# One weight load cut into transfers of 8, 8 and 112 partitions in a DMA-bound decode kernel

## The chip, the cores and the metric

The kernel runs on one core of a Trainium2 chip. The metric is the device time of the program in microseconds (us), the median of several executions. Each kernel was timed against the kernel before on the same chip.

The names in the profiles: PE is the matmul engine (PEld its weight loads), DVE, ACT and POOL are the vector, scalar and general engines, and SP is the engine that issues the loads here. The loads are carried out by the core's 16 DMA engines in packets, one contiguous row for one partition each: the trace of the kernel before has 15744 packets of 32 KB, 128 for each of its 123 loads of 4 MB, in sixteen rows in which one packet follows the other (from 165 to 200 us no gap is over 14 ns). SBUF is the memory on the chip that the loads write to, with 128 partitions. The DMA share is the mean busy share of the 16 DMA engines.

## The reference, cut to what matters

One token of a pre-LN decoder block with a cached attention of 32 heads and a dense layer behind it:

```python
B, Sq, D = 1, 1, 512
H, Sk, Dh = 32, 32768, 128          # k_cache, v_cache: [1, 32, 32768, 128] bf16
h  = x + attention(layernorm(x), k_cache, v_cache, wq) @ wo     # wo: [4096, 512] bf16, 4 MB
h2 = h + mish_mlp(layernorm(h), w1, b1, w2)
```

K and V are 537 MB of the 548 MB that are read. There is next to no reuse, so the kernel is a long stream of loads.

## The kernel before

SP issues all loads in one fixed order. K and V of a head come as 4 MB loads (128 partitions, 32 KB of contiguous memory for each); PE transposes K, multiplies, and frees the buffer for a later load. `wo` is loaded once, early, between a K and a V load, and stays.

```python
        def issue(ld):
            # ... src: 128 rows of up to 32 KB, dst: 128 partitions of the ring
            S.dma(SP, lambda: sp.dma_start(dst, src).then_inc(sems[ld.chan], 16), waits=ld.after)

            # ... in load_weights(which)
            elif which == "wo":
                S.dma(SP, lambda: sp.dma_start(
                    wo_sb[:, :, :], A_wo.rearrange("(h k) n -> k h n", k=128)).then_inc(sems["wo"], 16))
        # ...
        order = [(ld.pos, ld) for ld in loads]
        order += [(-1.0, "wqa"), (GH - 0.5, "wqb"), (GH + 2 * LAG + 0.2, "wo"),
                  (2 * GH + 2 * LAG + 0.2, "w12"), (1e9, "late")]
```

`wo_sb` has k, the place inside a head, on the partitions: partition k takes row k of each of the 32 heads, which are 32 pieces of 1 KB. On 16 engines that is 256 pieces for each. The first use of `wo` is in `y_init`, which PE reaches at 95 us, long after `wo` has landed at 77 us:

```python
            S.step(PE, lambda: t_.matmul(yrow[:, :], oneb[0:1, 0:1].to_broadcast([1, 128]), xrow[0:1, :], ...),
                   waits=["consts", ("xr", 16), ("wo", 16)])
```

Of the kernel before, what the change touches and what calls it, by code (L numbers as in the profile page):

```python
# [9 lines left out]
ALU = mybir.AluOpType  # L10
ACTF = mybir.ActivationFunctionType
AXX = mybir.AxisListType.X

PE, ACT, DVE, POOL, SP = "pe", "act", "dve", "pool", "sp"
# [7 lines left out]

W1A = 5
W2A = 6

LAG = 8

# [175 lines left out]
def build_kernel(nc, A_x, A_k_cache, A_v_cache, A_wq, A_wo, B_w1, B_b1, B_w2, out, NE=4):  # L203
# [21 lines left out]
    def sb(shape, dt, name):  # L225
        cm = nc.sbuf_tensor(name, shape, dt)
        t = cm.__enter__()
        allocs.append(cm)
        return t.ap()
# [9 lines left out]
    wo_sb = wo_flat.rearrange("p (h n) -> p h n", h=H)  # L239
# [28 lines left out]
    wbar = sb([128, 1], F32, "wbar")  # L268
# [51 lines left out]
    sems = {e: sem(f"ev_{e}") for e in (PE, ACT, DVE, POOL, SP)}  # L320
# [20 lines left out]
    def program(S):  # L341
        t_ = nc.tensor
        a = nc.scalar
        v = nc.vector
        g_ = nc.gpsimd
        sp = nc.sync
# [12 lines left out]
        def load_weights(which):  # L359
            if which == "wqa":  # L360
                S.dma(SP, lambda: sp.dma_start(  # L361
                    wqa, A_wq[:, 0:NH0 * Dh].rearrange("(p kc) n -> p kc n", kc=KC)).then_inc(sems["wqa"], 16))
            elif which == "wqb" and H > NH0:
                S.dma(SP, lambda: sp.dma_start(
                    wqb, A_wq[:, NH0 * Dh:HD].rearrange("(p kc) n -> p kc n", kc=KC)).then_inc(sems["wqb"], 16))
            elif which == "wo":
                S.dma(SP, lambda: sp.dma_start(
                    wo_sb[:, :, :], A_wo.rearrange("(h k) n -> k h n", k=128)).then_inc(sems["wo"], 16))
            elif which == "w12":
                S.dma(SP, lambda: sp.dma_start(  # L370
                    w1v[:, :, 0:W1A * 128],
                    B_w1.rearrange("(kc p) f -> p kc f", p=128)[:, :, 0:W1A * 128]).then_inc(sems["w1a"], 16))
            elif which == "late":
                S.dma(SP, lambda: sp.dma_start(
                    w1v[:, :, W1A * 128:F],
                    B_w1.rearrange("(kc p) f -> p kc f", p=128)[:, :, W1A * 128:F]).then_inc(sems["w1b"], 16))
                for a_, b_, s_ in ((0, W2A, "w2a"), (W2A, FJ - 1, "w2b")):
                    S.dma(SP, lambda a_=a_, b_=b_, s_=s_: sp.dma_start(
                        w2v[:, a_:b_, :],
                        B_w2[a_ * 128:b_ * 128, :].rearrange("(j p) n -> p j n", p=128)).then_inc(sems[s_], 16))  # L380
                S.dma(SP, lambda: sp.dma_start(
                    w2v[0:FLAST, FJ - 1, :], B_w2[(FJ - 1) * 128:F, :]).then_inc(sems["w2c"], 16))
# [4 lines left out]
        for _, ld in sorted(order, key=lambda o: o[0]):  # L387
            if isinstance(ld, str):
                load_weights(ld)
            else:  # L390
                issue(ld)
        S.dma(SP, lambda: sp.dma_start(out[0, 0, :].rearrange("(g n) -> g n", g=4), outsb[0:128:32, :]).then_inc(sems["out"], 16),
              waits=["fin"])
# [14 lines left out]
        for k, done in (("k", f"kf{NK - GH - 1}"), ("v", f"pv{NK - 2 * GH - 1}")):  # L408
            for x in range(NX):
# [22 lines left out]
               name="ident", waits=["iota"])  # L432
# [118 lines left out]
        def y_init():  # L551
            S.step(PE, lambda: t_.matmul(
                yrow[:, :], oneb[0:1, 0:1].to_broadcast([1, 128]), xrow[0:1, :], start=True, stop=False,
                skip_group_check=True), waits=["consts", ("xr", 16), ("wo", 16)])


        CV = (GH - LAG) * R
# [76 lines left out]

        hl = H - 1
        y_init()
        if H > NH0:
            S.wait(DVE, ["qT"])
        S.step(DVE, lambda: v.tensor_reduce(wbar[:, :], wo_sb[:, hl, :], AXX, ALU.add), waits=[("wo", 16)], name="wbar")
        S.step(DVE, lambda: v.tensor_scalar_mul(wbh[:, 0:1], wbar[:, :], 1.0 / D), name="wbh0", waits=["wbar"])  # L640
        S.step(DVE, lambda: v.scalar_tensor_tensor(
            wbh[:, 1:2], wbar[:, :], 1.0 / D, wbh[:, 0:1], ALU.mult, ALU.subtract), name="wbh", waits=["wbh0"])
# [3 lines left out]
        for t in range(GH):  # L646
            group(H, t)
            if t == LAG + 5:
                S.step(DVE, lambda: v.tensor_reduce(ysum[:, :], yrow[:, :], AXX, ALU.add), name="ysum",
                       waits=[f"yr{hl - 1}"])  # L650
                S.step(DVE, lambda: v.tensor_scalar_mul(MEANH, ysum[:, :], 1.0 / D), name="meanh", waits=["ysum"])

                for c in range(KC):
                    S.step(DVE, lambda c=c: v.tensor_tensor(
                        yrs[:, c * 128:(c + 1) * 128], yrow[:, c * 128:(c + 1) * 128], ident[:, :], ALU.mult),
                        waits=[f"yr{hl - 1}"], name=(f"yrs" if c == KC - 1 else None))
                S.step(DVE, lambda: v.tensor_reduce(
                    ycol[:, :], yrs[:, :].rearrange("p (c n) -> p c n", c=KC), AXX, ALU.add), name="ycol", waits=["yrs"])
            if t == LAG + 9:
                S.step(PE, lambda: t_.matmul(YC, ident[:, :], ycol[:, :], start=True, stop=False,  # L660
                                             skip_group_check=True), waits=["ycol"])
                S.step(PE, lambda: t_.matmul(T_b[0][:, 0:FP], b1r[:, :], identb[0:FP, 0:FP],
                                             is_transpose=True, start=True, stop=True),
                       name="b1t", waits=[("b1", 32), f"ev{NK - 2}", f"ev{NK - 1}"])
                S.step(DVE, lambda: v.tensor_copy(b1T[:, :], T_b[0][:, 0:FJ]), name="b1T", waits=["b1t"])
        for t in range(LAG):
# [5 lines left out]
            name="oT", waits=[f"pv{NK - 1}", f"o1s{hl}"])  # L672
        y_cols(hl)
        for s in range(2):
# [3 lines left out]
                waits=(["wbh"] if s == 0 else ()), name=("ym" if s == 1 else None))  # L678
        S.step(DVE, lambda: v.tensor_scalar(HC, YC, YM, MEANH, ALU.subtract, ALU.subtract),
               name="hc", waits=["ym"])  # L680
# [4 lines left out]
        for j in range(FJ):  # L685
            W = 128 if j < FJ - 1 else FLAST
            for kc in range(KC):
# [3 lines left out]
                    name=("hid" if j == FJ - 1 and kc == KC - 1 else None),  # L691
                    waits=(["xcT", ("w1a", 16), f"exq{H - 1}"] if j == 0 and kc == 0
                           else [("w1b", 16)] if j == W1A and kc == 0 else ()))
            if j == FJ // 2:
                S.step(PE, lambda: t_.matmul(V_REG, onesm[:, :], SSQ2, start=True, stop=True), name="v2",
                       waits=["ssq2"])
        S.step(ACT, lambda: a.activation(LNV2, V_REG, ACTF.Ln, bias=EPSC), name="ln2", waits=["v2"])
        S.step(ACT, lambda: a.activation(RSTD2, LNV2, ACTF.Exp, scale=-0.5), name="rstd2", waits=["ln2"])
        for c in range(KC):
# [5 lines left out]
               name="z", waits=["hid", "rstd2", "b1T"])  # L705
# [7 lines left out]
        for j in range(FJ):  # L713
            W = 128 if j < FJ - 1 else FLAST
            waits = ["act"] if j == 0 else []
            if j in (0, W2A, FJ - 1):
                waits.append(({0: "w2a", W2A: "w2b"}.get(j, "w2c"), 16))
            for c in range(KC):
# [3 lines left out]
                    name=("y2" if j == FJ - 1 and c == KC - 1 else None), waits=(waits if c == 0 else ()))  # L722
        S.step(DVE, lambda: v.tensor_copy(outsb[:, :], yps[:, HROW:HROW + 128]), name="fin", waits=["y2"])

    program(_Sched(nc, False, events, sems))
    with nc.Block() as blk:
        counts = {}
        for eng_name, attr in ((POOL, "gpsimd"), (SP, "sync"), (DVE, "vector"), (ACT, "scalar"), (PE, "tensor")):
            emitter = _Sched(nc, True, events, sems, only=eng_name)

            def _run(eng, emitter=emitter):
                program(emitter)
            getattr(blk, attr)(_run)
            counts.update(emitter.cnt)
        check = _Sched(nc, False, {}, sems)
        program(check)
        assert counts == check.cnt, (counts, check.cnt)
# [31 lines left out]
```

## Time and profile before

| | before |
|---|---|
| time, median | 1288.61 us (4 runs, 1288.39 to 1288.80) |
| DMA, mean over the span | 426 GB/s |
| PE, DVE busy | 80%, 59% |
| one 4 MB load in steady state | every 9.71 us |
| `wo`, 4 MB in 1 KB pieces | 11.85 us |
| last V landing, then to the end | 1277.35 us, then 9 us |

These are lines of the page of the kernel before: busy time by engine, the DMA share in 40 slices (tenths) and the rate in GB/s in the same slices, the summary of packets, the chain of work that ended last, and the issues of the large loads with their size and time to landing.

```profile
PE 1027.5 (80%) x25072; PEld 994.2 (77%) x25103; DVE 759.4 (59%) x1353; ACT 34.0 (3%) x134; POOL 2.7 (0%) x12
...
DMA  9999999999999999999999999999999999999998
GB/s 375 424 409 426 428 435 428 436 428 435 428 435 429 434 430 432 431 433 431 433 431 432 430 434 430 433 430 434 430 431 433 431 433 431 433 430 433 431 419 324
...
DMA 57%; PE 38%; DVE 3%; issue 1%; SPq 0%; ACT 0%
...
ring<-in_A_k_cache_dram SPq DMA_DIRECT2D x62, 4096.0 KB, 22.6
ring<-in_A_v_cache_dram SPq DMA_DIRECT2D x61, 4096.0 KB, 20.8
...
wo_sb<-in_A_wo_dram SPq DMA_DIRECT2D x1, 4096.0 KB, 36.8
```

The DMA slices are full from end to end, no compute engine is, and the rate is flat at about 431 GB/s: the loads bound the kernel. (The PE part of the chain is work that runs while the next loads arrive.) A load lands about 21 us after its issue at 9.7 us per load, so two are in hand all the time, and the engines are never short of work.

The columns after the stretch are busy us and instructions of each engine, then the granted PE clock, the DMA share and the rate in GB/s.

```profile
62.00:72.00 10.00, 6.66 (x153) 6.64 (x153) 4.51 (x8) 0.00 (x0) 0.00 (x0) 0.83 1.02 336
72.00:92.00 20.00, 6.54 (x159) 6.41 (x157) 4.27 (x8) 0.00 (x0) 0.00 (x0) 0.66 1.05 429
200.00:400.00 200.00, 163.24 (x4034) 158.26 (x4036) 122.10 (x213) 4.94 (x20) 0.00 (x0) 0.91 1.00 431
```

(The share can stand a little over 1, here 1.02 and 1.05: the records of packets overlap.) The first stretch holds most of `wo`: 4 MB in 11.85 us is 354 GB/s instead of 431; the 1 KB pieces cost 2.1 us. What SP did (start, duration, issue):

```profile
39.95 0.33 SPq L357 DMA_DIRECT2D ring<-in_A_k_cache_dram  x1
40.33 0.43 SPq L367 DMA_DIRECT2D wo_sb<-in_A_wo_dram  x1
46.21 24.93 SPq L357 DMA_DIRECT2D ring<-in_A_v_cache_dram  x1
71.18 0.43 SPq L357 DMA_DIRECT2D ring<-in_A_k_cache_dram  x1
```

The V issue behind `wo` stood for 24.9 us (the trace shows the time, not the reason). That was still in time: the first packets of V started at 74.1 us, and the last piece of `wo` ended at 76.6.

Each of these transfers leaves sixteen completion updates in the trace, as many as there are engines. I read them as one per engine (the fetch below moves one engine and one update by the same 1.6 us), and they show more than a landing time. In order of time, us, for three loads of the kernel before (worked out from the trace):

```
K before wo   62.79 62.86 62.87 63.02 63.03 63.04 63.25 63.26 64.38 64.47 64.51 64.55 64.67 64.73 65.29 65.31
V behind wo   84.36 84.39 84.40 84.56 84.60 84.82 84.85 85.93 86.08 86.13 86.17 86.25 86.27 86.81 86.84 87.58
last V        1272.05 1272.11 1272.12 1272.58 1272.72 1272.85 1273.73 1275.24 1275.44 1275.75 1275.95 1276.16 1276.57 1276.59 1277.34 1277.35
```

From V behind `wo` on, seven engines are early and nine late, by up to 5 us. The distance does not shrink in any later load (3.2 us from first to last update here, 4.8 after 180 us, 5.2 to 5.3 at the end): every engine is full. It grows with fetches of instructions: the trace counts 20 of 16 KB, 17 of them before 200 us, each a packet of 1.07 us (median) in the row of one engine. The updates before and after the fetch at 177.5 us differ by one engine that fell back from 3.2 to 4.8 us behind the first. In the row of packets the fetch takes 1.10 us and the 32 KB packet behind it 1.68 instead of 1.22, together the 1.6 us. That these fetches cause the rest of the lag is read from the times. A useful quantity follows: the mean of the sixteen updates of V behind `wo`, less the mean of K before `wo`, less 9.71 us for V itself, is what `wo` cost an engine on average. Before, it is 12.0 us (11.85 us and a share of the fetches).

### The profile page before, as it was taken

How to read it: one execution, taken by the hardware profiler on the slowest of the kernel's cores; microseconds unless marked ns; L12 is line 12 of the kernel's file. 1: busy time of each engine (PE TensorE's matmuls, PEld its weight loads, DVE VectorE, ACT ScalarE, POOL GpSimd, SP SyncE). 2: the span in 40 equal slices, each digit the busy share in tenths (PEclk: the TensorE clock that was granted, in tenths of full speed). 3: DMA queues.
4: the chain of work that ended last, by engine and by line, in shares of the span. 5: the costliest groups of instructions: out<-in, count | busy, mean ns of one | idle time of the engine just before them, and what ended most of it. 6: DMA issues, size and time to landing. Idle time of an engine off the chain costs nothing.

```text
span 1286.6 us, 52403 instructions
## 1 busy us (share of the span) xinstructions
PE 1027.5 (80%) x25072; PEld 994.2 (77%) x25103; DVE 759.4 (59%) x1353; ACT 34.0 (3%) x134; POOL 2.7 (0%) x12
## 2 busy tenths in 40 slices
PE   6858787788787788788888778888877887877886
PEld 6747787788787787777887777877777877777885
DVE  5635565566565565665666655655655655656663
ACT  0000000000000000000000000000000000000000
POOL 0000000000000000000000000000000000000000
PEclk8878989988899988988989988989989989989996
DMA  9999999999999999999999999999999999999998
GB/s 375 424 409 426 428 435 428 436 428 435 428 435 429 434 430 432 431 433 431 433 431 432 430 434 430 433 430 434 430 431 433 431 433 431 433 430 433 431 419 324
DMA packets 28800, 548.45 MB, mean 426 GB/s; under 512 B 2696, under 2 KB 9704, under 8 KB 10984
## 3 DMA queue, kind: packets, MB, share of 16 engines
q1 hardware_dynamic: 28680, 548.09, 99.7%
q8 instruction: 20, 0.33, 0.1%
q14 instruction: 4, 0.03, 0.0%
q0 software_dynamic: 96, 0.00, 0.0%
HBM read 548.08 MB, written 0.00 MB: 426 GB/s over the span
## 4 chain that ended last, share of the span: by engine, by line
DMA 57%; PE 38%; DVE 3%; issue 1%; SPq 0%; ACT 0%
DMA ring<-in_A_k_cache_dram 56%; PE tps L477 20%; PE sps L500 8%; PE ops L530 8%; DVE kt L488 2%; DMA ring<-in_A_v_cache_dram 2%; PE hlp L599 1%; DVE scb L580 1%; PE hlp L582 1%; DVE pmax L578 1%; PE hlp L587 1%; SPq L357 0%; PE sps L688 0%; PE yps L719 0%; SPq L361 0%
## 5 line engine op out<-in xcount | busy, mean ns | idle before, releaser
L488 DVE COPY kt<-tps 128x1024 bf16<-128x1024 bf16 x1024 | 707.8, 692 | 494.0 <-PE tps L477 486.9
L477 PE MATMUL tps<-identb,ring 128*128 128x128 bf16 x8192 | 693.7, 234 | 179.4 <-DMA ring<-in_A_k_cache_dram 176.1
L477 PEld LDWEIGHTS tps<-identb,ring 128*128 128x128 bf16 x8192 | 523.8, 104 | 188.4 <-DMA ring<-in_A_k_cache_dram 182.6
L530 PE MATMUL ops<-pbuf,ring 128*128 128x32 bf16 x8192 | 361.7, 178 | 57.2 <-DMA ring<-in_A_v_cache_dram 55.7
L500 PE MATMUL sps<-qcur,kt 128*128 128x32 bf16 x8192 | 376.0, 180 | 11.0 <-DVE scb L580 7.1
L500 PEld LDWEIGHTS sps<-qcur,kt 128*128 128x128 bf16 x8192 | 328.6, 99 | 18.7 <-DVE scb L580 14.4
L530 PEld LDWEIGHTS ops<-pbuf,ring 128*128 128x128 bf16 x8192 | 281.6, 97 | 70.1 <-DMA ring<-in_A_v_cache_dram 59.1
L590 ACT ACTIVATE pbuf<-scb,nbias 128x192 bf16<-128x192 f32 x32 | 14.6, 455 | 1164.8 <-PE ops L530 1094.8
L599 PE MATMUL hlp<-esum,onesf 128*128 128x1 f32 x128 | 18.6, 249 | 0.1
L599 PEld LDWEIGHTS hlp<-esum,onesf 128*128 128x128 f32 x128 | 16.8, 190 | 0.0
L578 DVE TENSOR_REDUCE pmax<-sps 128x1 f32<-128x256 f32 x32 | 13.3, 415 | 0.5 <-PE sps L500 0.5
L580 DVE COPY scb<-sps 128x256 f32<-128x256 f32 x32 | 13.3, 415 | 0.0
L582 PE MATMUL hlp<-ident,pmax 128*1 128x128 f32 x64 | 13.1, 289 | 0.1
L594 ACT ACTIVATE pbuf<-scb,nbias 128x64 bf16<-128x64 f32 x32 | 11.1, 348 | 60.2 <-PE ops L530 60.2
L587 PE MATMUL hlp<-gmax,onesr 1*128 1x1 f32 x64 | 12.1, 256 | 0.1
L617 DVE TENSOR_SCALAR o1s<-ops,rtot 128x1 f32<-128x1 f32 x32 | 6.7, 210 | 8.0 <-PE ops L530 8.0
L587 PEld LDWEIGHTS hlp<-gmax,onesr 1*128 1x128 f32 x64 | 9.4, 182 | 1.2 <-DVE gmax L585 0.2
L607 DVE COPY qcur<-qT 128x1 bf16 (+1 forms) x63 | 9.3, 147 | 0.0
L585 DVE TENSOR_REDUCE gmax<-hlp 1x1 f32<-1x128 f32 x32 | 8.6, 270 | 0.2
L621 DVE SCALAR_TENSOR_TENSOR ocur<-ops,rtot,o1s 128x1 bf16<-128x1 f32 x31 | 6.6, 213 | 0.7 <-PE ops L530 0.7
L443 PE MATMUL hlp<-xnT,ring 128*128 128x1 bf16 x128 | 3.7, 164 | 3.1 <-issue 3.1
L443 PEld LDWEIGHTS hlp<-xnT,ring 128*128 128x128 bf16 x128 | 3.6, 99 | 3.2 <-issue 3.2
(85 smaller groups left out, 55.2 us busy)
## 6 DMA issues: line engine op xcount, KB each, us to landing
ring<-in_A_k_cache_dram SPq DMA_DIRECT2D x62, 4096.0 KB, 22.6
ring<-in_A_v_cache_dram SPq DMA_DIRECT2D x61, 4096.0 KB, 20.8
ring<-in_A_v_cache_dram SPq DMA_DIRECT2D x9, 1024.0 KB, 19.8
ring<-in_A_k_cache_dram SPq DMA_DIRECT2D x5, 1024.0 KB, 15.5
wo_sb<-in_A_wo_dram SPq DMA_DIRECT2D x1, 4096.0 KB, 36.8
ring<-in_A_wq_dram SPq DMA_DIRECT2D x1, 3584.0 KB, 30.4
ring<-in_A_k_cache_dram SPq DMA_DIRECT2D x1, 2048.0 KB, 12.1
ring<-in_A_v_cache_dram SPq DMA_DIRECT2D x1, 2048.0 KB, 21.2
```

Source lines behind the costliest of these rows:

```text
L477: S.step(PE, lambda r=r: t_.matmul(tb[:, r * 128:(r + 1) * 128], block("k", i, r), identb[:, :], is_transpose=True, start=True, stop=True) ...
L488: dve(i, lambda: v.tensor_copy(kt[:, i % NE, :], T_b[i % 2][:, :]), f"ev{i}", waits)
L500: S.step(PE, lambda r=r, c=c: t_.matmul(S_b[:, c:c + WIDE], kt[:, i % NE, r * 128:(r + 1) * 128], q.to_broadcast([128, WIDE]), start=True, ...
L530: S.step(PE, lambda r=r, c=c: t_.matmul(ob[:, 0:WIDE], block("v", i, r), pbuf[:, c:c + 1].to_broadcast([128, WIDE]), start=(r == 0 and g i ...
L578: dve(i, lambda: v.tensor_reduce(pmax[:, :], S_b[:, 0:NCOL], AXX, ALU.max), f"pmax{hs}", [f"qkb{hs}"])
L580: dve(i, lambda: v.tensor_copy(scb[:, :], S_b[:, 0:NCOL]), f"sc{hs}", [])
L582: S.step(PE, lambda: t_.matmul(A_REG, pmax[:, :], ident[:, :], start=True, stop=True), name=f"A{hs}", waits=[f"pmax{hs}"] + (["qT" if H > ...
L587: S.step(PE, lambda: t_.matmul(B_REG, onesr[0:1, :], gmax[0:1, :], start=True, stop=True), name=f"B{hs}", waits=[f"gmax{hs}"], priv=pe_cha ...
L590: S.step(ACT, lambda: a.activation(pbuf[:, 0:CV], scb[:, 0:CV], ACTF.Exp, bias=nb[:, :], scale=SC, accum_out=esum[:, 0:1]), name=f"exp{hs} ...
L594: S.step(ACT, lambda: a.activation(pbuf[:, CV:NCOL], scb[:, CV:NCOL], ACTF.Exp, bias=nb[:, :], scale=SC, accum_out=esum[:, 1:2]), name=f"e ...
L599: S.step(PE, lambda s=s: t_.matmul(C_REG, onesf[:, :], esum[:, s:s + 1], start=(s == 0), stop=(s == 1)), name=(f"C{hs}" if s else None), w ...
L607: S.step(DVE, lambda j=j, n=n: v.tensor_copy(qcur[:, j:j + 1], qT[:, n:n + 1] if S.round is None else qT[:, bass.ds(S.round + (3 - j), 1)] ...
```

## The change

Its intent rests on a premise that the kernel before does not show: eight partitions are moved by eight engines, both times the same eight, and 112 evenly by all sixteen. Two transfers of eight partitions then give eight engines 64 pieces more, and the 112 partitions left give each of the sixteen 32 pieces fewer. The texts call these eight the lower engines and the others the upper ones; these are only names for the two halves. If the late engines are the other eight, they gain 32 pieces of 46 ns, 1.5 us (an estimate, from 11.85 us for 256 pieces). Nothing else changes; the diff, with its context cut and two equal edits of the waits shown as one:

```diff
+WOP = 16
@@
             elif which == "wo":
-                S.dma(SP, lambda: sp.dma_start(
-                    wo_sb[:, :, :], A_wo.rearrange("(h k) n -> k h n", k=128)).then_inc(sems["wo"], 16))
+                for p0, p1 in [(p, p + 8) for p in range(0, WOP, 8)] + [(WOP, 128)]:
+                    S.dma(SP, lambda p0=p0, p1=p1: sp.dma_start(
+                        wo_sb[p0:p1, :, :],
+                        A_wo.rearrange("(h k) n -> k h n", k=128)[p0:p1]).then_inc(sems["wo"], 16))
@@ y_init and the reduction of wo_sb[:, hl, :] (wbar)
-                waits=[... ("wo", 16)]
+                waits=[... ("wo", 16 * (WOP // 8 + 1))]
```

More of the change, by code (lines that the diff above doesn't have):

```diff
@@ L553, in y_init @@
                 yrow[:, :], oneb[0:1, 0:1].to_broadcast([1, 128]), xrow[0:1, :], start=True, stop=False,
-                skip_group_check=True), waits=["consts", ("xr", 16), ("wo", 16)])
+                skip_group_check=True), waits=["consts", ("xr", 16), ("wo", 16 * (WOP // 8 + 1))])
         CV = (GH - LAG) * R
@@ L638, in program @@
             S.wait(DVE, ["qT"])
-        S.step(DVE, lambda: v.tensor_reduce(wbar[:, :], wo_sb[:, hl, :], AXX, ALU.add), waits=[("wo", 16)], name="wbar")
+        S.step(DVE, lambda: v.tensor_reduce(wbar[:, :], wo_sb[:, hl, :], AXX, ALU.add), waits=[("wo", 16 * (WOP // 8 + 1))], name="wbar")
         S.step(DVE, lambda: v.tensor_scalar_mul(wbh[:, 0:1], wbar[:, :], 1.0 / D), name="wbh0", waits=["wbar"])
```

## The prediction

> **What bounds the kernel now.** The DMA engines. The page's slices show them at nine tenths or more all but the last slice, 426 GB/s on average, with PE busy 80% and DVE 59%; the chain of waits is 57% DMA. In steady state one 4 MB load lands every 9.71 us. Each transfer has sixteen completion updates in the trace, one per engine. They show two groups: at the load that lands around 222 us seven come within 0.5 us and nine 2.6 to 4.8 us after the first; at the last value load they come at 1272.05-1273.73 (seven) and 1275.24-1277.35 us (nine). The lag comes from instruction fetches: the table of queues counts 20 of 16 KB; 17 of them lie before 180 us, and each costs the engine that serves it about 1.5 us, never caught up, because every engine is always full. The last value update, 1277.35 us, starts the tail (9 us to the end). So the time is the work of the slowest engine. Perfect balance would give about 2.5 us.
>
> **What the change does.** SP issues two transfers more (0.43 us each, SP has time); the bytes are the same. [...] wo took 11.85 us for 256 pieces of 1 KB per engine, 46 ns each. Lower engines get 288 pieces (+1.5 us), upper ones 224 (-1.5 us). That is the intent: if the fetches burden the upper half, it takes 1.5 us from the late engines. One late engine (2.6 us, delayed by other fetches) would be in the lower half, so the gain would be only 0.6 us.
>
> **Why I expect a loss.** [...] One engine here already moves 32 KB in 1.213 us, 27 GB/s[...]. From the early group's 1272.05-1273.73 us, and the one late lower engine, the last value update moves to about 1281-1283 us: +5 us; if the lower half is the late one, +8 us. All of it lies on the critical path.
>
> **Time:** 1294 us, 8 in 10 between 1287 and 1298.5. Chances: faster by over 2% 0.01, within 2% 0.97, slower 0.02.
>
> **What would show it.** [...]the 1 KB packets of the first two transfers last or stand about 150 ns apart per engine instead of 46; the first two transfers complete about 10 us after the load before them, on eight engines; afterwards eight updates of each load stay some 5 to 9 us behind the others; the last value update at 1281-1283 us; tail unchanged. [...]
>
> **What would make it wrong.** [...]starving of the upper engines[...].

Passages of this text and of the expectations below are cut, and each cut is marked. Terms of the forecast's sum went with them. The sum was: the eight lower engines need 20 us for `wo` instead of 11.85, +8.2 us, and stay late. Of the 20 us, 10.3 are 224 pieces of 46 ns, and the rest is a time that I assumed for the two small transfers, because I took eight neighbouring partitions to be slow together. The early group's last update, 1273.73 us, and 8.2 us give the 1281 to 1283 us of the text, +5 us. If neighbours are not slow, 1287.5 to 1290 us; and, as a risk, 1 to 2 us more if the 112 partitions are slow too.

## The result, and the profile after

| | before | after |
|---|---|---|
| time, median of 4 | 1288.61 us | 1302.16 us (1300.98 to 1302.30) |
| ratio | | 1.0102, 95% interval 1.0087 to 1.0117 |
| what `wo` cost an engine on average | 12.0 us | 22.9 us |
| last V landing | 1277.35 us | 1290.09 us |

Ratios are the mean time of one kernel's runs over that of the other's of the same rounds, so not quite the ratio of the medians. The change costs 13.5 us by the medians; in the two profiled executions (1288.37 and 1300.98 us) it is 12.6 us.

The page of the kernel after, the same lines:

```profile
PE 1032.2 (79%) x25103; PEld 996.8 (77%) x25103; DVE 759.3 (58%) x1353; ACT 34.0 (3%) x134; POOL 2.7 (0%) x12
...
DMA  9999999999999999999999999999999999999997
GB/s 375 412 265 425 431 431 431 431 434 432 431 430 435 432 430 430 435 432 431 430 435 431 431 431 434 432 431 431 434 432 431 431 433 433 432 430 433 432 418 313
...
DMA 57%; PE 38%; DVE 3%; issue 1%; SPq 0%; ACT 0%
...
ring<-in_A_k_cache_dram SPq DMA_DIRECT2D x62, 4096.0 KB, 22.4
ring<-in_A_v_cache_dram SPq DMA_DIRECT2D x61, 4096.0 KB, 20.1
...
wo_sb<-in_A_wo_dram SPq DMA_DIRECT2D x1, 3584.0 KB
...
wo_sb<-in_A_wo_dram SPq DMA_DIRECT2D x2, 256.0 KB
```

One slice of forty is different: the third, 65 to 97 us, falls from 409 to 265 GB/s. The DMA share of that slice is still full. This is the line to learn from: the engines were busy, but their packets took longer (89 ns for the median 1 KB packet of `wo`, 51 before). A hole in the share, as the 0.22 of e3 below, would have meant missing work; a full share at a lower rate means slow work. By stretches, after:

```profile
62.00:72.00 10.00, 4.50 (x104) 4.40 (x101) 2.77 (x5) 0.00 (x0) 0.00 (x0) 0.83 1.05 172
72.00:92.00 20.00, 5.46 (x127) 5.25 (x122) 4.21 (x7) 0.00 (x0) 0.00 (x0) 0.72 1.11 257
200.00:400.00 200.00, 165.11 (x4035) 159.71 (x4033) 121.85 (x214) 5.39 (x22) 0.00 (x0) 0.90 1.00 432
```

172 GB/s in the first ten us against 336, then 257 against 429 in the next twenty, and from 200 us on the same rate as before. These two deficits add up to 5.1 MB, 11.8 of the 12.6 us at 431 GB/s, so nearly all of the loss is made between 62 and 92 us, and it is never made good. SP, after:

```profile
39.62 0.33 SPq L359 DMA_DIRECT2D ring<-in_A_k_cache_dram  x1
39.99 16.39 SPq L371 DMA_DIRECT2D wo_sb<-in_A_wo_dram  x3
56.42 23.44 SPq L359 DMA_DIRECT2D ring<-in_A_v_cache_dram  x1
79.91 0.43 SPq L359 DMA_DIRECT2D ring<-in_A_k_cache_dram  x1
```

The completion updates of `wo` after the change, all three transfers together, and those of V behind it:

```
wo            40.49 40.89 66.24 66.39 66.75 67.27 67.54 68.92 69.19 69.39 69.56 69.58 70.07 70.39 70.89 71.91 72.82 73.19
              82.15 82.94 83.12 83.26 84.21 84.36 84.63 85.48 86.36 86.86 87.10 88.10 89.05 89.24 89.48 91.25
V behind wo   95.44 95.54 95.67 95.95 96.12 96.28 96.96 97.18 97.46 97.79 98.07 98.41 98.82 98.99 99.32 100.75
```

There are 34 updates, not 48: two at once after the issues (40.49 and 40.89 us) and 32 landings, which is 8 + 8 + 16. The kernel waits for a count of 48, and it was reached with these 34. Eight landings for each small transfer, where each full one has sixteen: so I read that the small transfers run on eight engines, as meant, and both are through by 73.19 us. But the 112 partitions then take until 82 to 91 us, on all sixteen engines. On average an engine spent 22.9 us on `wo`, 10.8 more than before; not just eight of them.

### The profile page after: what moved, and what is told of

Same layout as the page of the kernel before. It is cut to its first block, busy times and chain, and to the rows that moved or that the text cites. A ratio compares the mean times of both kernels' runs of the same rounds, so it can differ in the third digit from the quotient of the medians.

```text
span 1299.2 us, 52436 instructions
## 1 busy us (share of the span) xinstructions
PE 1032.2 (79%) x25103; PEld 996.8 (77%) x25103; DVE 759.3 (58%) x1353; ACT 34.0 (3%) x134; POOL 2.7 (0%) x12
## 4 chain that ended last, share of the span: by engine, by line
DMA 57%; PE 38%; DVE 3%; issue 1%; SPq 0%; ACT 0%
DMA ring<-in_A_k_cache_dram 56%; PE tps L482 20%; PE sps L505 8%; PE ops L535 8%; DVE kt L493 2%; DMA ring<-in_A_v_cache_dram 2%; PE hlp L604 1%; PE hlp L587 1%; DVE scb L585 1%; DVE pmax L583 1%; PE hlp L592 1%; PE yrow L552 1%; SPq L359 0%; PE sps L693 0%; PE yps L724 0%
## 5 line engine op out<-in xcount | busy, mean ns | idle before, releaser
L592 PE MATMUL hlp<-gmax,onesr 1*128 1x1 f32 x64 | 12.1, 256 | 0.1
L552 PE MATMUL yrow<-wo_sb,ocur 128*128 (+1 forms) x31 | 11.7, 377 | 0.0
```

The source lines that it names most:

```text
L552: S.step(PE, lambda: t_.matmul(yrow[:, :], ocur[:, 0:1].to_broadcast([128, 128]), rhs, start=False, stop=(h == H - 2), skip_group_check=Tr ...
L592: S.step(PE, lambda: t_.matmul(B_REG, onesr[0:1, :], gmax[0:1, :], start=True, stop=True), name=f"B{hs}", waits=[f"gmax{hs}"], priv=pe_cha ...
```

## The experiments

Theory P (place): the side that is written is the limit, and which partitions a transfer writes decides its rate. A few neighbouring partitions are slow together, the same number spread out are not, and shapes other than the full 128 partitions can be slow as well. When the runs were planned this was an assumption. The rivals: L or Q, the load on half of the engines holds up the queue for the others; N, more transfers cost more by themselves; H, the reading of short rows of `wo` is the slow side. (Q is L for the 112: they are slow only because the small transfers are ahead of them.)

Most kernels are the kernel before with this edit, and differ in one line, the list of pieces (partitions, first and last head):

```diff
+WO_PIECES = [...]
             elif which == "wo":
-                S.dma(SP, lambda: sp.dma_start(
-                    wo_sb[:, :, :], A_wo.rearrange("(h k) n -> k h n", k=128)).then_inc(sems["wo"], 16))
+                wsrc = A_wo.rearrange("(h k) n -> k h n", k=128)
+                for ps, h0, h1 in WO_PIECES:
+                    S.dma(SP, lambda ps=ps, h0=h0, h1=h1: sp.dma_start(
+                        wo_sb[ps, h0:h1, :], wsrc[ps, h0:h1, :]).then_inc(sems["wo"], 16))
```

(and `16 * len(WO_PIECES)` in the two waits). All results below are timed in three rounds unless said otherwise; the kernel before stood at 1288.5 to 1288.7 us throughout.

### e1_16_112: sixteen partitions and 112, meant for all engines in both

```diff
+WO_PIECES = [(slice(0, 16), 0, 32), (slice(16, 128), 0, 32)]
```

> wo by one transfer of 16 partitions and one of 112, each on all sixteen engines[...], so every engine has its 256 pieces as before and no engine of the lower half has more. Theory P[...]: [...]1297 to 1303 us. Theory L (the load on the lower half and the queue it holds up): 1288.6 us, within 1 us.

Measured: 1301.42 us, ratio 1.0098 (1.0081 to 1.0115). That every engine carries what it carried before, here and in e2, was the plan of the run and an assumption: no trace names an engine, and landings on all sixteen are seen for the 112 alone, in the change. The loss is that of the change. Its stretches, the first while most engines were at the sixteen partitions, the second in the 112:

```profile
64.00:70.00 6.00, 1.57 (x27) 1.57 (x28) 0.50 (x1) 0.00 (x0) 0.00 (x0) 0.76 0.91 113
72.00:82.00 10.00, 6.10 (x153) 5.90 (x150) 4.90 (x8) 0.00 (x0) 0.00 (x0) 0.90 1.12 210
```

If the plan held, the load on half of the engines is not needed for the loss: L alone falls. The sixteen partitions go at 113 GB/s. The 112 go at 210 GB/s, slower than I had counted on (354, the rate of `wo` before).

### e2_halves: two transfers of 64 partitions

```diff
+WO_PIECES = [(slice(0, 64), 0, 32), (slice(64, 128), 0, 32)]
```

> wo by two transfers of 64 partitions, each on all sixteen engines[...], again 256 pieces per engine. Theory P: [...]1295 to 1297 us. Theory L: 1288.6 us, within 1 us.

Measured: 1299.04 us, ratio 1.0082 (1.0065 to 1.0099); 2 us above my range. Its stretch in the middle of the two transfers:

```profile
66.00:82.00 16.00, 9.86 (x208) 9.66 (x208) 6.29 (x10) 0.00 (x0) 0.00 (x0) 0.79 1.12 204
```

204 GB/s, against 354 for `wo` in one transfer. The median 1 KB packet took 89 ns instead of 51. My range was low because the rate that I had assumed for it was above 204.

### e3_heads_spread: the load of the change, on spread partitions

```diff
+WO_PIECES = [(slice(0, 128), 0, 28)] + [(slice(b + p, b + 32, 4), 28, 32) for b in range(0, 128, 32) for p in range(4)]
```

> 28 of the 32 heads of wo for all 128 partitions in one transfer, the last four heads by sixteen transfers of eight partitions that lie four apart (0, 4, ... 28): the lower engines get 288 pieces and the upper ones 224, as in the change[...]. Theory P: no loss beyond the shift of 1.5 us; 1287 to 1290.5 us. Theory L: the load and the queue are those of the change and there are more transfers; 1297 us or more.

Measured: 1294.04 us, ratio 1.0045 (1.0028 to 1.0061). Neither range holds it. The trace tells why:

```profile
70.00:74.00 4.00, 3.66 (x101) 3.46 (x96) 3.03 (x6) 0.00 (x0) 0.00 (x0) 1.00 1.02 330
74.00:80.00 6.00, 0.00 (x0) 0.00 (x0) 0.44 (x1) 0.00 (x0) 0.00 (x0) 0.84 0.22 69
```

and SP's row of it, all 17 issues of `wo` and the V load behind them:

```profile
39.50 40.54 SPq L371 DMA_DIRECT2D wo_sb<-in_A_wo_dram  x17
80.08 0.44 SPq L359 DMA_DIRECT2D ring<-in_A_v_cache_dram  x1
```

A DMA share of 0.22: the engines were idle. Each spread transfer took SP about 0.7 us to issue, they stood in front of the V load, and V was issued at 80.08 us when the engines had run dry at 74. This is the other kind of loss, a hole, and not the one of the change. The pieces themselves ran well: the median 1 KB packet is 48 ns (51 before). Most of these belong to the 28 heads at full height, but the pieces that ran in the hole, from 74 to 80 us, took 46 ns as well. I read no more than that from this run.

### e4_heads_next: the same with neighbouring partitions

```diff
+WO_PIECES = [(slice(0, 128), 0, 28)] + [(slice(p, p + 8), 28, 32) for p in range(0, 128, 8)]
```

> The same as the run before it, but each of the sixteen small transfers takes eight neighbouring partitions (0 to 7, 8 to 15, ...)[...]. Theory P: [...]2 to 6 us more than the spread one, 1290 to 1296 us. Theory L: as the spread one, within 1 us.

Measured: 1291.08 us, ratio 1.0016 (1.0000 to 1.0033). It is faster than the spread one, against the expectation of P, because a transfer of neighbouring partitions was issued in 0.30 us and no hole arose:

```profile
74.00:78.00 4.00, 0.86 (x25) 0.76 (x21) 1.24 (x2) 0.00 (x0) 0.00 (x0) 1.00 1.11 285
```

The share is full (1.11) and the rate low, the sign of packets that take longer, but mild: 59 ns for the median packet in 73 to 78 us. Why it is milder than in e7 below, 138 ns, is not shown. As a comparison of times the pair failed; e7 and e11 below make it without the issue cost.

### e5_three_full: three transfers, all over 128 partitions

```diff
+WO_PIECES = [(slice(0, 128), 0, 2), (slice(0, 128), 2, 4), (slice(0, 128), 4, 32)]
```

> Control for the number of transfers: wo by three transfers of 256, 256 and 3584 KB, as many and as large as in the change, but each over all 128 partitions (2, 2 and 28 heads). Theory P[...]: 1288.5 us, within 1 us. Rival N (two small transfers ahead cost by themselves, by issue or completion): a good part of the 13.5 us, 1295 us or more.

Measured: 1288.81 us, ratio 1.0003 (0.9986 to 1.0019), and 12.1 us for `wo` on an average engine. Three transfers of the sizes of the change cost nothing. N falls.

### e6_112_only: only the 112 partitions (a wrong result on purpose)

```diff
+WO_PIECES = [(slice(16, 128), 0, 32)]
+        S.step(POOL, lambda: g_.memset(wo_sb[0:16, :, :], 0.0), name="woz")   # wo's transfer waits for it
```

> Wrong result on purpose: only the 112-partition transfer of wo, the other sixteen partitions are set to zero. Theory P[...] at the rate seen in the change and in the 16 + 112 run (about 213 GB/s): 3.67 MB take 17.2 us instead of 11.85; 1293 to 1295 us. Rival Q (the 112 are slow in the change only because the two eight-partition transfers hold up the queue of half of the engines, so that the others wait): 224 pieces of 46 ns, 10.4 us; 1287 us.

Measured: 1295.02 us, ratio 1.0054 (1.0037 to 1.0071), at the upper end of P. It moves less than the kernel before and is 6.4 us slower. An average engine spends 16.6 us on it, where 224 pieces at 46 ns are 10.4 us. Its stretch in the middle of the transfer:

```profile
68.00:80.00 12.00, 8.46 (x202) 8.19 (x200) 6.03 (x10) 0.00 (x0) 0.00 (x0) 0.86 1.15 252
```

So the 112 are slow by themselves, with no eight-partition transfer in front: Q falls as the cause of this part, which is about half of the loss. One thing besides the transfer differs: the clearing (13.7 us on POOL) delays the start. The load two before `wo` lands 1.6 us later than in the kernel before on average (55.49 against 53.92 us), and some 1.6 of the 6.4 us belong to that. The 16.6 us are counted from a later load and don't contain it.

### e7_8s_only and e11_8s_spread_only: only two transfers of eight partitions (wrong results on purpose)

Both clear `wo_sb` first, as e6 does. They differ in the partitions alone: 0 to 7 and 8 to 15, or every fourth of 0 to 31 and of 32 to 63. Size, number of engines, pieces and transfers are the same, and the clearing delays both alike (0.8 and 1.0 us two loads before `wo`).

```diff
e7   +WO_PIECES = [(slice(0, 8), 0, 32), (slice(8, 16), 0, 32)]
e11  +WO_PIECES = [(slice(0, 32, 4), 0, 32), (slice(32, 64, 4), 0, 32)]
```

> Wrong result on purpose: only the two eight-partition transfers of wo (0.5 MB), everything else of wo set to zero. [...]64 pieces take 3 us on the lower engines and nothing on the upper ones: about 1277.5 us. Theory P: 8 to 10 us on the lower engines: 1282 to 1285 us. Together with the 112-only run: if the two costs simply add up, this run's lower engines and that run's excess give the 13.5 us of the change.

> Wrong result on purpose, to set beside the run with only the two eight-partition transfers (1284.66 us): the same two transfers of eight partitions and 256 KB on the lower eight engines, everything else of wo zero, but the partitions lie four apart (0, 4, ... 28 and 32, 36, ... 60)[...]. Theory P: 64 pieces at 46 ns, 3 us instead of about 8 to 10; 1277 to 1280 us. If eight-partition transfers are slow for any other reason (half of the engines, small transfers): 1284.7 us, within 1 us.

Measured: e7 1284.66 us, ratio 0.9970 (0.9954 to 0.9987); e11 1279.05 us, ratio 0.9925 (0.9910 to 0.9940). The stretch of e7:

```profile
64.00:72.00 8.00, 4.04 (x95) 3.67 (x91) 2.77 (x4) 0.00 (x0) 0.00 (x0) 0.82 1.02 157
```

and of e11:

```profile
64.00:72.00 8.00, 6.55 (x185) 6.38 (x183) 4.89 (x8) 0.00 (x0) 0.00 (x0) 1.00 1.03 422
```

Both shares are full; 157 GB/s against 422. The median 1 KB packet takes 138 ns (64 to 70 us) in e7 and 46 ns in e11. Nothing but the choice of partitions (and with it of the rows of `wo` that are read) is left to explain 5.6 us: eight neighbouring partitions are slow. The 512 pieces of e7 take 125 ns on average, 8.0 us for the 64 of each of the eight engines, at the lower end of the 8 to 10 that I had assumed.

But the trace of e7 shows more than theory P says. While the pieces run, eight engines carry 32 KB packets of K and V end to end, with no piece between them. The sixteen of these packets that start between 63.5 and 68 us take 2.6 to 3.5 us (median 3.07); in e11 all 44 that start in this stretch take 1.21 to 1.29 us. The slow pieces therefore also hold up engines that carry none of them. By which path is not shown. All sixteen engines lose: in order of time, the updates of V behind `wo` come 3.9 to 5.7 us later in e7 than in e11. A held-up packet counts as busy, so the DMA share does not show this.

The costs add up. Per engine on average, `wo` costs 16.6 us in e6 and 6.0 us in e7, 22.6 together; the change has 22.9. No further term is needed for what the 112 and the small transfers do to each other.

### e8_k_halves: the same with whole 32 KB rows

```diff
             if ld.chan == "kown5":
+                for p0, p1 in [(0, 64), (64, 128)]:
+                    S.dma(SP, lambda p0=p0, p1=p1: sp.dma_start(dst[p0:p1], src[p0:p1]).then_inc(sems[ld.chan], 16))
```

(and a count of 32 where this load is waited for; `wo` as before)

> wo as before; instead the sixth K load of the first head (4 MB, whole 32 KB rows) comes by two transfers of 64 partitions. Theory P (the side that is written): [...]its packets take 2.4 us instead of 1.21; 1297.5 to 1299.5 us. Rival H (the slow side is the reading of wo's 1 KB rows, 128 KB apart): no change, 1288.5 us, packets of 1.21 us.

Measured: 1299.65 us, ratio 1.0087 (1.0070 to 1.0104), just above the range of P. Its stretch over the two transfers:

```profile
18.00:34.00 16.00, 6.21 (x120) 6.06 (x116) 5.45 (x8) 0.00 (x0) 0.00 (x0) 0.72 0.98 202
```

A 32 KB packet takes 1213 to 1221 ns in the kernel before (10th to 90th percentile, 16 to 1200 us); in this stretch the median is 2558 ns. Twice as long, with contiguous rows and nothing about `wo`. H falls: short rows are not the cause.

### e9_k_112: 112 and 16 with whole 32 KB rows

As e8, with `[(16, 128), (0, 16)]`.

> wo as before; the sixth K load of the first head (32 KB rows) by one transfer of the partitions 16 to 127 and one of 0 to 15[...]. Theory P: the seven packets per engine of the first[...] near 2 us on average, as 213 GB/s in the change says; the one packet per engine of the second[...] about 5 us; 22 us for both instead of 9.7, so about 1300.5 us (1299 to 1302). If the losses came from the reading of wo's short rows: 1288.5 us and packets of 1.21 us.

Measured: 1298.61 us, ratio 1.0078 (1.0062 to 1.0093), a little under my range. In the 112 the median packet takes 2.03 us, in the sixteen 3.6 us (none of these is 1.21):

```profile
16.00:26.00 10.00, 5.68 (x128) 5.43 (x128) 5.36 (x8) 0.00 (x0) 0.00 (x0) 1.00 1.00 257
```

The sixteen came out shorter than the 5 us expected (at e1's 113 GB/s, sixteen packets of 32 KB side by side would take 4.6 us, an estimate). The engines arrive at them spread over more than 3 us and overlap with the 112; whether that is why was not tested. In the 112 the packets run from 1.7 to 2.3 us (10th to 90th percentile), between the 1.21 of a full load and the 2.56 of e8's halves. The run doesn't tell why. Which partitions each engine takes in a 112-partition transfer can't be read from this trace; it has no engine and no partition of a packet.

### e10_spread_later and e12_spread_no_hole: is the intended gain to be had?

The pieces are those of e3, but the sixteen spread transfers come later in SP's order: behind the V load (e10), or behind the K load after that one (e12).

```diff
e10  +(GH + 2 * LAG + 8.7, "wo_rest")
e12  +(2 * GH + 1.0, "wo_rest")
```

> What the change wanted, [...]without the hole of the earlier spread run: 28 heads of wo in one transfer, then the V load behind it, and only then the sixteen spread transfers of the last four heads on the lower half, at a time when the queue has two loads in hand. If the lower half is the early one and balance is to be had this way: 1286.5 to 1288.3 us, the two groups of completions closer by up to 3 us. [...] If the sixteen issues starve the queue again: above 1292 us.

> The spread version once more without its hole: in the run before it the DMA share fell to 0.71 in 82 to 84 us because the K load behind the sixteen small transfers was issued late (83.75 us). Here that K load is issued ahead of the sixteen, and the V load behind them has until 94 us. If shifting 32 pieces per engine to the lower half helps when [...]nothing starves: 1286.5 to 1288.2 us. If some of the late engines are in the lower half (the run with only the spread transfers says three of eight were among the late ones when wo came), they become later by 1.5 us and set the time[...]: 1289 to 1291.7 us. No third cause expected; above 1292 us would be a hole again.

Measured in five rounds each: e10 1291.75 us, ratio 1.0026 (1.0012 to 1.0039), which lies in none of my ranges; e12 1291.08 us, ratio 1.0018 (1.0004 to 1.0032), in its second range. The last V updates of e12:

```
1275.42 1275.75 1275.77 1275.95 1276.15 1276.36 1276.64 1277.31 1277.34 1277.44 1277.49 1277.52 1277.53 1277.54 1280.18 1280.30
```

Fourteen engines are now within 2.1 us of each other, which is closer than before, and two are 2.6 us behind them and set the time. The runs don't tell how much of that is the shift. The name of e12 is not earned: SP's issues stalled (the sixteen took it from 71.17 to 93.91 us), V was issued at 93.95 us, and from 92 to 96 us the rate was 303 GB/s. This is what the two profiles show there, first e10 (82 to 84 us), then e12:

```profile
82.00:84.00 2.00, 0.00 (x0) 0.00 (x0) 0.00 (x0) 0.00 (x0) 0.00 (x0) 0.50 0.71 282
92.00:96.00 4.00, 1.70 (x49) 1.59 (x46) 1.72 (x3) 0.00 (x0) 0.00 (x0) 1.00 0.97 303
96.00:98.00 2.00, 0.00 (x0) 0.00 (x0) 0.00 (x0) 0.00 (x0) 0.00 (x0) 0.63 1.03 289
```

Only e10 has a clear hole. In e12 the share is nearly full at a low rate: the 32 KB packets that start from 94 to 100 us take 1.8 us (median) instead of 1.21, and from 84 to 90 us they do so in e10. All 512 spread pieces run after 92 us in e12 (after 82 us in e10), and the later half of them goes to the partitions 64 to 127 while a full load writes there too. Whether that is why the packets take longer was not tested. On average an engine finishes its last V 2.5 us later than before (mean of the updates 1277.17 against 1274.66), so the loss is not only the two that stay behind. A cleaner version of the shift was not found.

A hint why two stay behind is in e11, where eight engines got 2.96 us of extra pieces and eight none, in front of the same V load (updates of K before and V behind):

```
K  63.84 63.92 63.94 64.05 64.22 64.28 64.33 64.36 64.41 64.86 64.87 65.09 65.53 65.71 65.92 65.98
V  74.05 74.13 75.23 75.43 75.61 75.63 75.65 75.68 76.51 76.60 76.63 76.72 76.91 77.55 77.56 77.74
```

Taking 9.71 + 2.96 us off the last eight of V gives 63.84, 63.93, 63.96, 64.05, 64.24, 64.88, 64.89 and 65.07, within 0.03 us of eight values of K. So, if these eight updates are those of the engines with the extra pieces, at this time the eight engines with the extra pieces were the five earliest and three that were already 1.0 to 1.2 us behind the first. The premise that this half is early held for five of the eight. That the stragglers of e10 and e12 come from the other three is an inference; no run names an engine.

## Why the prediction was wrong

The direction was right, and so was the slowness of eight neighbouring partitions; who pays for it, the cost of the 112 partitions and the time were not: 1302.16 us against 1294 and a range up to 1298.5.

- **DMA bounds the kernel, and an engine's delay is never made good.** Right. The rate from 200 us on is 431 GB/s before and 432 after, and the time from the last V landing to the start of the output's issue is 7.1 us before and 7.0 after.
- **Eight neighbouring partitions are slow.** Right, though it was an assumption when I wrote it: by the packets of e7 the two transfers take 8.0 us on the engines that carry them, where 64 pieces of 46 ns are 3.0, the time that they take in e11 with spread partitions. The sign named beforehand, packets about 150 ns apart, came as 138 ns in e7.
- **The step that failed** is in the sum of 20 us for `wo` on the lower engines (above), together with "upper ones 224 (-1.5 us)". It failed in two places. First, I gave the 112-partition transfer the piece time of a 128-partition one, 46 ns, and counted it as a gain of 1.5 us for all engines. Alone, in e6, it takes 16.6 us per engine, not 10.4. I had named slow 112 partitions only as a risk of 1 to 2 us more; they cost about 6 us, and on all sixteen engines. Second, I let the two small transfers cost only the engines that carry them. In e7 the other eight lose about 5 us too. With these figures `wo` takes 8.0 + 16.6 = 24.6 us on the engines with the small transfers and some 21.6 us on the others; 22.9 were measured on average.
- **"Afterwards eight updates of each load stay some 5 to 9 us behind the others"** was wrong for both reasons. All sixteen were late: 11.8 us on average at V behind `wo` (10.8 by the measure above, because the K load before it already ended 1.0 us later, beside the first pieces), and 11.7 at the last V (mean of its updates 1274.66 before, 1286.37 after). The last engine trails this mean by 3.7 us instead of 2.7, which gives 12.7 us at the last V landing (1277.35 to 1290.09).
- **"Starving of the upper engines"**, named as a risk, is nearer to what happened than I thought. The upper engines were not starved: the share stayed full (1.05 and 1.11). But in e7 the engines without a piece were held up, 3.07 us for a packet of 1.21.
- **The intended gain**, 0.6 us by my count, can't be seen at all in the change, and two attempts at the shift with every fourth partition (e10, e12) ended at +3.0 and +2.4 us. A hole (e10) and slowed packets of the load beside the pieces (both) came with the shift, so that they don't decide whether the shift itself would gain.

What stays open: how the 112 partitions are dealt to the engines, hence why they go at 210 GB/s in e1, 252 in e6 and 257 in e9; how slow pieces hold up engines that carry none; and which engines are the late ones. By which mechanism the choice of partitions acts is not shown either; measured are 204 GB/s for 64 partitions, 113 for 16, and 46 ns a packet for spread ones. One rival is untested: each partition keeps its row of the source, so every choice of partitions also chose the rows that are read together, and no run changed one without the other. What the runs show directly is that the choice of partitions decides.

No version with a right result beat the kernel before; e7 and e11 are faster only because they load an eighth of `wo`.

## What to carry to other kernels

Where DMA is the bound, keep large SBUF loads at all 128 partitions and cut them along the free dimension instead: three full-height transfers cost nothing (e5, ratio 1.0003), two of 64 partitions cost 10.5 us for 4 MB (e2), and a cut at 16 cost 13 (e1). In a profile, separate two kinds of low rate: a DMA share that falls (a late issue, as in e3: 0.22) and a share that stays full (packets that take longer, as in the change: 1.05 and 1.11); they have different cures. When a load is reshaped to balance engines, price the remainder too: here the part that was meant to get cheaper brought half of the loss. And price the neighbours: in e7 a slow small transfer made the loads on the other engines take 3.07 us for a packet of 1.21.
